# Seven half-size products per pair of token tiles in the second layer's first matmul, and an integer form of the float64 weight decoding

## Chip, cores and metric

One core of a Trainium2 chip runs the whole program. The metric is the time of one execution in device microseconds; the kernel before takes 967.71 us (median of 3 runs, 967.36 to 967.76).

## What is computed

Threshold attention over 4 batches of 8 heads, sequence 576, head size 64, and then two layers on the 2304 x 512 result. The second layer, which the change rewrites, is

```python
h = x @ w_in                                   # 2304x512 @ 512x1024
e = np.exp(h - h_max)
solu = h * (e / (np.sum(e, axis=-1, keepdims=True) + 1e-09))
ln = (solu - mu) / np.sqrt(var + 1e-06) * g_ln  # mu, var: over the 1024 columns of a token
return (ln @ w_out).astype(np.float32)          # 2304x1024 @ 1024x512
```

All four weight matrices arrive as float64 and are turned into float32 on the chip.

## The kernel before, in words

Every matmul operand is kept as a rounded part `hi` and a remainder `lo`, and a product is hi·hi + hi·lo + lo·hi: three matmuls. Their splitting is a copy on ACT and a subtraction on POOL (in a few places on DVE). Each engine works through its own list in the order in which the program text issues it (a hand-written order); between engines only semaphores wait.

**Attention** (until about 360 us) goes through 144 units; weight blocks of 128 x 512 are decoded in between as "jobs", advanced a step at a time by `Jobs.step` (letter J in the table `ORDER`). **Decoding** a block is `words_to_f32` (L506 to L531): the two 32-bit words of a float64 are turned into float32 by one instruction on ACT (L512), five on DVE (L514, L517, L520, L524, L527) and one float addition on POOL (L531). There are 48 blocks; the first 8 go beside attention, 40 beside the first layer.

**First layer** (360 to 757 us): 4 groups of 4 rows of blocks over 5 chunks of tokens (three of 512 columns, two of 384), 80 steps of `moe1_in` (L793) and `moe1_out` (L833), the second 2 steps behind the first. DVE, ACT and POOL clip, square and split each step's result (`moe1_act`), `store_y` adds a finished chunk into `x` (L844), and the jobs load weights of the next group, of which `w_in2` goes partly, `w_out2` wholly, through a float32 copy in DRAM.

**Second layer** (757 us on): 18 token tiles of 128, one after the other. `moe2_in(i)` is 48 matmuls of 512 columns (4 row blocks, 3 matmuls, 2 halves of the 1024 columns; L877) into two PSUM banks. `moe2_ln(i)` reads these banks: DVE takes the row maximum of each half (L893), ACT the two exponentials (L897), DVE multiplies and sums (L905), ACT squares and sums (L910), DVE and POOL (L913) form the inverse deviation, DVE scales (L917). Then the tile is transposed: `moe2_shuffle` does blocks on DVE (L932) and the rest by five DMAs through DRAM, `moe2_land` splits what came back (L951, L952); tiles 0 and 17 go through TensorE instead (`moe2_tr`, L964, `ON_PE`). `moe2_out(i)` is 24 matmuls (L988), one bank, an ACT copy (L992) and a store. In the middle the order is in(i+3), out(i), in(i+4), out(i+1), and so on (the list `seq`):

```python
    seq = [("out", 0)]
    for i in range(1, NTT - 3):
        seq += [("in", i + 3), ("out", i)]
    seq += [("out", NTT - 3), ("tr", NTT - 1), ("out", NTT - 2), ("out", NTT - 1)]
```

Of the kernel before, what the change touches and what calls it, by code (L numbers as in the profile page):

```python
# [21 lines left out]
def kernel(  # L22
# [16 lines left out]
    P = 128  # L39
# [56 lines left out]
    ON_PE = (0, NT // P - 1)  # L96
# [3 lines left out]
    EVERY = (3, 3, 3, 2, 2, 2)  # L100
    X_LEAD = 2
    IN2_AHEAD = (2,)
# [403 lines left out]
    def words_to_f32(raw, n, got):  # L506
# [3 lines left out]
        au, cu = a.bitcast(U32), upper  # L510
        c = cu.bitcast(F32)
# [13 lines left out]
        if fine[0]:  # L525
            yield 1, "b"
# [95 lines left out]
    def block(key, n):  # L622
# [5 lines left out]
        if what == "in2":  # L628
            return (w_in2_f if n in IN2_AHEAD else w_in2)[rows, cols]
# [125 lines left out]
    x_t = {}  # L755

# [101 lines left out]
    def y_split(c, kk):  # L858
        if kk == 0:
            tag = f"x{4 - c % 2 if c else 2}"  # L860
            x_t["y", c] = [xs_p.tile([P, KD, YT * P], F32R, tag=tag + t, name="y") for t in ("h", "l")]
        hi, lo = (t[:, kk, :] for t in x_t["y", c])
        xv = x[:, kk, c * YT * P : (c + 1) * YT * P]
        nc.scalar.copy(hi, xv)
        nc.gpsimd.tensor_tensor(lo, xv, f32(hi), op=ALU.subtract)

    def moe2_in(i):
        r = slice(i % YT * P, i % YT * P + P)
        yh, yl = (t[:, :, r] for t in x_t["y", i // YT])
        ps = [bank("h", (turns[0] + n) % NHB, "h") for n in ((1, 2) if i % 2 else (0,))]  # L870
        if i % 2 == 0:
            ps.append(y_bank(0, "h"))
        n = 0
        for kk in range(KD):
            for a, s in ((yh, 0), (yh, 1), (yl, 0)):
                for g in range(2):
                    nc.tensor.matmul(  # L877
                        ps[g], lhsT=a[:, kk, :], rhs=wg_t["in2", g][s][:, kk, :],
                        start=(n < 2), stop=(n >= 6 * KD - 2),
                    )  # L880
                    n += 1
        h2_ps[i] = ps

    def moe2_ln(i):
        ps = h2_ps.pop(i)
        st = g_p.tile([P, 10], F32, tag="st", name="st", bufs=2)
# [284 lines left out]
```

## Time and profile before

| | |
|---|---|
| median of 3 runs | 967.71 us |
| the profiled execution, its span | 968.04 us, 966.3 us |
| PE busy (5299 matmuls) | 944.8 us, 98% |
| DVE / ACT / POOL busy | 74% / 51% / 62% |
| attention, first layer, second layer | about 360, 397 and 209 us |

Shares of busy time are means over the three stages; the rows below are by stage, and where one number stands for many rows the row is that of a view that groups them.

### The profile page before, as it was taken

How to read it: one execution, taken by the hardware profiler on the slowest of the kernel's cores; microseconds unless marked ns; L12 is line 12 of the kernel's file. 1: busy time of each engine (PE TensorE's matmuls, PEld its weight loads, DVE VectorE, ACT ScalarE, POOL GpSimd, SP SyncE). 2: the span in 40 equal slices, each digit the busy share in tenths (PEclk: the TensorE clock that was granted, in tenths of full speed). 3: DMA queues.
4: the chain of work that ended last, by engine and by line, in shares of the span. 5: the costliest groups of instructions: out<-in, count | busy, mean ns of one | idle time of the engine just before them, and what ended most of it. 6: DMA issues, size and time to landing. Idle time of an engine off the chain costs nothing.

```text
span 966.3 us, 15184 instructions
## 1 busy us (share of the span) xinstructions
PE 944.8 (98%) x5299; PEld 842.3 (87%) x5299; DVE 711.9 (74%) x1132; ACT 493.9 (51%) x924; POOL 603.3 (62%) x575
## 2 busy tenths in 40 slices
PE   7999999999999989999999999999999999999998
PEld 7899899999989978889888988898889988888886
DVE  5788888788788875898678876888675676666562
ACT  3667677777767675354333433333334444344433
POOL 7678788888978898677445544654547614334422
PEclk9999999999999999999999999999999999999999
DMA  6665666657666314211311131112311124444443
GB/s 144 148 147 124 152 159 145 170 126 176 157 142 154 81 44 98 68 66 44 120 44 66 44 119 45 65 45 77 129 34 45 44 66 131 109 120 124 138 119 90
DMA packets 89726, 99.61 MB, mean 103 GB/s; under 512 B 50000, under 2 KB 62608, under 8 KB 89648
## 3 DMA queue, kind: packets, MB, share of 16 engines
q1 hardware_dynamic: 87952, 97.97, 38.5%
q8 instruction: 42, 0.69, 0.3%
q10 hardware_dynamic: 1696, 0.66, 0.3%
q14 instruction: 36, 0.29, 0.1%
HBM read 55.13 MB, written 15.88 MB: 73 GB/s over the span
## 4 chain that ended last, share of the span: by engine, by line
PE 79%; POOL 8%; issue 4%; DVE 4%; ACT 3%; DMA 1%; ACTq 0%; POOLq 0%; DVEq 0%
PE y L833 18%; PE h L793 18%; PE o L988 10%; PE h L877 10%; PE av L453 9%; PE zt L403 6%; PE sc L326 6%; POOL plo L430 3%; PE tr L271 1%; POOL wg L560 1%; DMA nat<-in_q_dram 1%; DVE mcol L339 1%; POOL dec_a L531 1%; POOL xl L769 1%; ACT phi L429 1%
## 5 line engine op out<-in xcount | busy, mean ns | idle before, releaser
L430 POOL TENSOR_TENSOR plo<-e,phi 128x576 fp32r<-128x576 f32 x144 | 207.6, 1451 | 48.9 <-ACT phi L429 48.8
L816 POOL TENSOR_TENSOR gl<-cl,gh 128x512 fp32r<-128x512 f32 (+1 forms) x80 | 100.3, 1254 | 160.0 <-ACT gh L815 85.3
L793 PE MATMUL h<-xh,wg 128*128 128x512 f32 (+1 forms) x640 | 184.1, 369 | 0.7 <-DVE e L421 0.7
L833 PE MATMUL y<-gh,wg 128*128 128x512 f32 (+1 forms) x640 | 184.6, 369 | 0.0
L421 DVE SCALAR_TENSOR_TENSOR e<-zt,ntau,e 128x576 f32<-128x576 f32 x144 | 117.3, 815 | 54.5 <-ACT e L416 34.8
L793 PEld LDWEIGHTS h<-xh,wg 128*128 128x128 f32 x640 | 118.4, 188 | 16.7 <-DVE e L421 1.0
L833 PEld LDWEIGHTS y<-gh,wg 128*128 128x128 f32 x640 | 118.5, 188 | 15.9
L416 ACT ACTIVATE e<-zt 128x576 f32<-128x576 f32 x144 | 93.9, 652 | 70.0 <-PE zt L403 53.2
L339 DVE TENSOR_REDUCE mcol<-sc 128x1 f32<-128x576 f32 x160 | 116.7, 748 | 4.9 <-PE sc L326 4.7
L833 PE MATMUL y<-gl,wg 128*128 128x512 f32 (+1 forms) x320 | 118.8, 371 | 0.9 <-POOL gl L816 0.9
L793 PE MATMUL h<-xl,wg 128*128 128x512 f32 (+1 forms) x320 | 117.8, 368 | 0.0
L815 ACT CAST gh<-cl 128x512 fp32r<-128x512 f32 (+1 forms) x80 | 46.3, 579 | 111.9 <-DVE cl L814 110.7
L812 ACT ACTIVATE cl<-cl,half 128x512 f32<-128x512 f32 (+1 forms) x80 | 54.4, 679 | 95.4 <-DVE cl L811 95.4
L988 PE MATMUL o<-wg,ln 128*128 128x512 f32 x432 | 102.7, 393 | 0.0
L877 PE MATMUL h<-wg,y 128*128 128x512 f32 x432 | 101.1, 390 | 0.0
L988 PEld LDWEIGHTS o<-wg,ln 128*128 128x128 f32 x432 | 80.9, 188 | 18.8 <-ACT ln L951 0.4
L429 ACT CAST phi<-e 128x576 fp32r<-128x576 f32 x144 | 96.2, 668 | 1.5 <-ACT mt L369 0.7
L952 POOL TENSOR_TENSOR ln<-land,ln 128x1024 fp32r<-128x1024 f32 x16 | 38.5, 2404 | 91.7 <-ACT ln L951 85.0
L877 PEld LDWEIGHTS h<-wg,y 128*128 128x128 f32 x432 | 81.0, 188 | 16.8
L811 DVE TENSOR_SCALAR cl<-h 128x512 f32<-128x512 f32 (+1 forms) x80 | 50.6, 632 | 51.1 <-PE h L793 49.0
L326 PE MATMUL sc<-k_both,q_st 128*128 128x288 f32 x320 | 72.2, 307 | 6.5 <-issue 1.8
L403 PE MATMUL zt<-q_st,k_both 128*128 128x288 f32 x320 | 72.4, 308 | 1.6 <-DVE lo L280 1.3
(114 smaller groups left out, 1883.2 us busy)
## 6 DMA issues: line engine op xcount, KB each, us to landing
raw<-in_moe_w_in_dram SPq DMA_DIRECT2D x24, 512.0 KB
raw<-in_moe_w_out_dram SPq DMA_DIRECT2D x24, 512.0 KB
k_both<-q_st SPq DMA_DIRECT2D x30, 288.0 KB
sq<-so SPq DMA_DIRECT2D x64, 128.0 KB
land<-sq SPq DMA_DIRECT2D x16, 512.0 KB
k_both<-lo SPq DMA_DIRECT2D x32, 144.0 KB
q_st<-lo SPq DMA_DIRECT2D x32, 144.0 KB
x<-xs SPq DMA_DIRECT2D x32, 144.0 KB
```

Of the source, the lines that this page charges most:

```text
L326: nc.tensor.matmul(ps[:, c, 0:HS], lhsT=st[j][i][r, n * P : n * P + P], rhs=kk[j][i][r, o + c * HS : o + (c + 1) * HS], start=(st is q_st) ...
L339: nc.vector.tensor_reduce(mc[:, n : n + 1], sc_ps.pop((h, n))[:, :, 0:HS], axis=AXES.XY, op=ALU.max, negate=True)
L403: nc.tensor.matmul(ps[:, c, 0:HS], lhsT=st, rhs=mv[:, c * HS : (c + 1) * HS], start=(m == 0), stop=(m == len(todo) - 1),)
L416: nc.scalar.activation(out=e, in_=st_ps[u][:, :, 0:HS], func=ACTF.Exp)
L421: nc.vector.scalar_tensor_tensor(out=e, in0=st_ps.pop(u)[:, :, 0:HS], scalar=ntau[:, 0:1], in1=e, op0=ALU.is_ge, op1=ALU.mult)
L429: nc.scalar.copy(hi, e)
L430: (nc.vector if u - NU in LO_DVE or u < NU - UNITS and u % UNITS in LO_UNITS else nc.gpsimd).tensor_tensor(lo, e, f32(hi), op=ALU.subtract)
L793: nc.tensor.matmul(ps, lhsT=a[:, kk, f], rhs=m[:, kk, :], start=(n == 0 and kk == 0), stop=(n == 2 and kk == KD - 1),)
L816: nc.gpsimd.tensor_tensor(gl, cl, f32(gh), op=ALU.subtract)
L833: nc.tensor.matmul(y_ps[c][d], lhsT=a[:, jj, ds_], rhs=m, start=(jj == 0 and n == 0), stop=(jj == JG - 1 and n == 2),)
L877: nc.tensor.matmul(ps[g], lhsT=a[:, kk, :], rhs=wg_t["in2", g][s][:, kk, :], start=(n < 2), stop=(n >= 6 * KD - 2),)
L988: nc.tensor.matmul(ps, lhsT=a[:, f, :], rhs=wg_t["out2", f // 4][m][:, f % 4, :], start=(n == 0), stop=(n == len(terms) - 1))
```

## The change

In the second layer two neighbouring token tiles form a 2 x 2 block matrix: rows by tile, columns by halves of the 512 inputs; `w_in2` is cut in the same way into B11, B12, B21, B22. The Winograd form of Strassen's scheme gives the pair's four results from seven products of a 128 x 256 by a 256 x 512 block, 6 matmuls each, with sums of blocks as operands.

- `op_rows` reads `w_in2` (all of it now decoded ahead into DRAM) and forms three of its blocks and four sums of them, each split into hi and lo: 8 subtractions on DVE, 14 copies on ACT, 14 subtractions on POOL, in the first layer's last group. `out2` is split later than before.
- `y_adds` forms four sums of blocks of `x` per pair (DVE); `y_split` splits four pieces per pair, 1792 columns in place of 1024.
- `product(k, n)` is one of the seven. They add up in three banks; the partial results 1, 5 and 6 are copied out by ACT, after 2, 3 and 7 DVE adds the bank to such a copy and takes the row maximum in the same instruction, and after 4 it takes the maximum from the bank. So a later product on a bank waits for ACT or DVE to have read it.
- `moe2_ln` finds three of a pair's four halves in SBUF instead of PSUM. Tiles 1 and 16 go through TensorE too. All operands lie in one large tile `xs` cut by offsets; the order is written out by hand for pairs 0 to 2 and the tail, with a loop for pairs 3 to 8.
- Decoding is now two instructions on ACT, three on DVE and one addition of 32-bit integers on POOL.

```diff
-    ON_PE = (0, NT // P - 1)
+    ON_PE = (0, 1, NT // P - 2, NT // P - 1)
...
-        nc.vector.tensor_scalar(au, au, 3, 0x3FFFFFF8, op0=ALU.logical_shift_left, op1=ALU.bitwise_and)
+        nc.vector.tensor_scalar(au, au, 3, None, op0=ALU.logical_shift_left)
+        nc.scalar.activation(out=lower.bitcast(F32), in_=lower, func=ACTF.Copy, bias=2.0, scale=2.0 ** -51)
...
         nc.vector.scalar_tensor_tensor(
-            out=au, in0=upper, scalar=0xC0000000, in1=au, op0=ALU.bitwise_and, op1=ALU.bitwise_or
-        )
-        yield 1, "s"
-        nc.vector.tensor_scalar(cu, au, 0xFF800000, None, op0=ALU.bitwise_and)
...
-        nc.vector.scalar_tensor_tensor(
-            out=c, in0=lower, scalar=2.0 ** -52, in1=c, op0=ALU.mult, op1=ALU.mult
+            out=au, in0=upper, scalar=0x80000000, in1=au, op0=ALU.bitwise_and, op1=ALU.bitwise_xor
         )
...
-        nc.gpsimd.tensor_tensor(a, a, c, op=ALU.add)
+        nc.gpsimd.tensor_tensor(au, au, lower, op=ALU.add)
...
+    def y_adds(k):
+        r0, r1, pairs = y_views(k)
+        a11, a12, a21, a22 = (x[:, h : h + KH, r] for r in (r0, r1) for h in (0, KH))
+        s1, s2, s3, s4 = (t[:, h : h + KH, :] for t in pairs for h in (0, KH))
+        nc.vector.tensor_tensor(s1, a21, a22, op=ALU.add)
+        nc.vector.tensor_tensor(s3, a11, a21, op=ALU.subtract)
+        nc.vector.tensor_tensor(s2, s1, a11, op=ALU.subtract)
+        nc.vector.tensor_tensor(s4, a12, s2, op=ALU.subtract)
...
+    PRODUCTS = {
+        1: (0, 0, B11), 2: (1, 1, B21), 3: (2, 5, B22), 4: (0, 6, T4), 5: (2, 2, T1), 6: (0, 3, T2), 7: (0, 4, T3),
+    }
...
+    def add_max(i, g, ps):
+        h = so_half(i, g)
+        nc.vector.tensor_tensor_reduce(
+            out=h, in0=ps, in1=h, scale=1.0, scalar=-3.0e38, op0=ALU.add, op1=ALU.max, accum_out=maximum(i, g)
+        )
+
+    def product(k, n):
+        b, a, o = PRODUCTS[n]
+        hi, lo = y_t[k, a]
+        w = op_tile(o)
+        ps = acc(k, b)
+        first = n in (1, 2, 5)
+        for kk in range(KH):
+            for m, (st, at_) in enumerate(((hi, kk), (hi, KH + kk), (lo, kk))):
+                nc.tensor.matmul(
+                    ps, lhsT=st[:, kk, :], rhs=w[:, at_, :],
+                    start=first and kk == 0 and m == 0, stop=kk == KH - 1 and m == 2,
+                    skip_group_check=not first,
+                )
...
+    for k in range(3, NPR):
+        o = 2 * k - 4
+        last = k == NPR - 1
+        if k > 3:
+            product(k - 1, 7)
+        ln_step(o + 2)
+        moe2_fetch(o + 2)
+        product(k, 1)
+        moe2_store(o - 1)
+        product(k, 5)
+        product(k, 2)
+        product(k - 1, 4)
+        moe2_land(o + 1)
+        ln_step(o + 3)
...
+        ln_step(o + 3)
+        if not last:
+            y_adds(k + 1)
+        ln_step(o + 3)
+        moe2_fetch(o + 3)
+        if not last:
+            for m in range(4):
+                y_split(k + 1, m)
+        if k > 3:
+            moe2_out(o)
+            product(k, 6)
+        product(k, 3)
+        moe2_store(o)
+        moe2_land(o + 2)
+        ln_step(2 * k)
...
+        ln_step(2 * k)
+        moe2_out(o + 1, slice(12 * last, None))
```

DVE's list before, one tile of the second layer (`h` a PSUM half, `st` columns of statistics, `so` the tile's result):

```order
L893 TENSOR_REDUCE st<-h 128x1 x2
L894 TENSOR_TENSOR st<-st 128x1
L901 TENSOR_SCALAR st<-st 128x1
L902 RECIPROCAL st<-st 128x1
L905 SCALAR_TENSOR_TENSOR so,st<-h,st,so 128x512 x2
L909 TENSOR_SCALAR st<-st 128x1
L912 TENSOR_SCALAR st<-st 128x1
L914 TENSOR_SCALAR st<-st 128x1
L915 TENSOR_SCALAR st<-st 128x1
L916 TENSOR_TENSOR st<-st 128x1
L917 TENSOR_SCALAR so<-so,st 128x1024
L932 STREAM_TRANSPOSE so<-so 128x8x4x32
```

DVE's list after, in the loop, from `add_max` behind product 2 into the odd tile's `moe2_ln` (`ISA` is the adding and maximum instruction and the read of its result, `mx` the maxima, `x` the sums of `y_adds`):

```order
L975 ISA so,mx<-h,so 128x512
L975 ISA mx 128x1
L1006 TENSOR_REDUCE mx<-h 128x1
L1015 TENSOR_SCALAR st<-mx 128x1
L1022 TENSOR_SCALAR st<-st 128x1
L1023 RECIPROCAL st<-st 128x1
L1026 SCALAR_TENSOR_TENSOR so,st<-h,st,e 128x512
L1026 SCALAR_TENSOR_TENSOR so,st<-so,st,e 128x512
L1030 TENSOR_SCALAR st<-st 128x1
L938 TENSOR_TENSOR x<-x 128x2x128
L939 TENSOR_TENSOR x<-x 128x2x128
L940 TENSOR_TENSOR x<-x 128x2x128
```

Of a pair's four maxima three have moved into adding instructions, and the four sums stand between the odd tile's L1030 and its next step (L1033); the even tile's remaining steps go on as before.

PE's list after, one turn of the loop from product 1 of pair 6 to its product 7 (`h_9486` is the bank of pair 5's product 4, `o` an output bank):

```order
L987 MATMUL h_9664<-op_8137,xs_5363 128x512 x6
L987 MATMUL h_9676<-op_8162,xs_5363 128x512 x6
L987 MATMUL h_9684<-op_8182,xs_5363 128x512 x6
L987 MATMUL h_9486<-xs_5363 128x512 x6
L1132 MATMUL o_9739<-xs_5363,ln_8707 128x512 x24
L987 MATMUL h_9664<-op_8202,xs_5363 128x512 x6
L987 MATMUL h_9676<-op_8222,xs_5363 128x512 x6
L1132 MATMUL o_9795<-xs_5363,ln_8995 128x512 x16
L1132 MATMUL o_9795<-xs_5363,ln_8996 128x512 x4
L1132 MATMUL o_9795<-xs_5363,ln_8997 128x512 x4
L987 MATMUL h_9664<-op_8247,xs_5363 128x512 x6
```

Where 24 matmuls of one tile alternated with 24 of an output, products 1, 5, 2, the pair before's 4, an output, 6, 3, an output and 7 follow each other; product 4 shares its bank with product 7, 24 matmuls earlier.

POOL's list at the end of attention, before and then after (`plo` the attention's remainders, `gl` and `xl` or `xs` those of the first layer, `dec_a` and `wg` a decoded block and its remainder):

```order
L430 TENSOR_TENSOR plo<-e,phi 128x576 x6
L500 TENSOR_TENSOR x<-x,rb 128x576
L430 TENSOR_TENSOR plo<-e,phi 128x576 x2
L531 TENSOR_TENSOR dec_a<-dec_a,raw 128x512
L560 TENSOR_TENSOR wg<-dec_a,wg 128x512
L816 TENSOR_TENSOR gl<-cl,gh 128x512
L769 TENSOR_TENSOR xl<-x,xh 128x512 x2
```

```order
L429 TENSOR_TENSOR plo<-e,phi 128x576 x6
L499 TENSOR_TENSOR x<-x,rb 128x576
L429 TENSOR_TENSOR plo<-e,phi 128x576 x2
L873 TENSOR_TENSOR gl<-cl,gh 128x512
L826 TENSOR_TENSOR xs<-x,xs 128x512 x2
```

The last decoded block's two instructions no longer stand here; with fewer steps in a job all eight blocks are through earlier in attention.

## Rows read from the trace of the kernel before

**Rows 1.** Busy time by stretch: span and busy us (instructions) per engine, TensorE clock, DMA.

```profile
360.00:757.70 397.70, 396.12 (x1909) 347.60 (x1910) 302.85 (x441) 158.65 (x273) 236.94 (x183) 1.00 0.22 69
800.00:940.00 140.00, 140.00 (x614) 114.89 (x613) 88.19 (x211) 59.10 (x118) 52.46 (x40) 1.00 0.46 123
```

**Rows 2.** Chain of waits, second layer: start us, us, what, number of matmuls.

```profile
763.21 2.10 PE y L833 x12
...
784.71 5.54 PE o L988 x24
790.25 5.44 PE h L877 x24
```

**Rows 3.** Timeline, second layer, PE: start us, us, engine, what.

```profile
823.03 5.61 PE L877 MATMUL h<-wg,y 128*128 128x512 f32 x24
```

**Rows 4.** Timeline, DVE, one tile from maximum to the next maximum.

```profile
834.30 1.25 DVE L893 TENSOR_REDUCE st<-h 128x1 f32<-128x512 f32 x2
835.58 0.16 DVE L894 TENSOR_TENSOR st<-st 128x1 f32<-128x1 f32 x1
837.32 0.21 DVE L901 TENSOR_SCALAR st<-st 128x1 f32<-128x1 f32 x1 [1.58 <-ACT so L897]
...
839.24 0.21 DVE L909 TENSOR_SCALAR st<-st 128x1 f32<-128x1 f32 x1
840.82 0.15 DVE L912 TENSOR_SCALAR st<-st 128x1 f32<-128x1 f32 x1 [1.37 <-ACT so L910]
...
842.20 0.58 DVE L916 TENSOR_TENSOR st<-st 128x1 f32<-128x1 f32 x1
...
843.66 1.25 DVE L932 STREAM_TRANSPOSE so<-so 128x1024 f32<-128x1024 f32 x1
844.83 1.25 DVE L893 TENSOR_REDUCE st<-h 128x1 f32<-128x512 f32 x2
```

**Rows 5.** A POOL instruction beside it, and durations (min/median/max ns) of two DVE lines.

```profile
841.75 1.02 POOL L865 TENSOR_TENSOR y<-x,y 128x384 fp32r<-128x384 f32 x1
...
L916 DVE TENSOR_TENSOR st<-st x18: 159/568/580, 773.3 to 947.9; 128x1 f32<-128x1 f32 x18
L917 DVE TENSOR_SCALAR so<-so,st x18: 811/814/1476, 773.5 to 948.1; 128x1024 f32<-128x1024 f32 x18
```

**Rows 6.** Durations by line, min/median/max ns.

```profile
L905 DVE SCALAR_TENSOR_TENSOR so<-h,st,so x36: 745/750/753, 767.5 to 944.1; 128x512 f32<-128x512 f32 x36
L844 DVE TENSOR_TENSOR x<-x,y x60: 544/686/690, 489.3 to 775.6; 128x512 f32<-128x512 f32 x36, 128x384 f32<-128x384 f32 x24
L769 DVE TENSOR_TENSOR xl<-x,xh x4: 1165/1186/1929, 354.3 to 360.6; 128x512 fp32r<-128x512 f32 x4
L556 DVE TENSOR_SCALAR wf<-wf,g_sb x8: 582/830/1242, 736.3 to 762.2; 128x512 f32<-128x512 f32 x8
L531 POOL TENSOR_TENSOR dec_a<-dec_a,raw x48: 1296/1330/1830, 77.3 to 738.4; 128x512 f32<-128x512 f32 x48
```

**Rows 7.** Timeline, a tile's last way through DRAM.

```profile
938.83 1.25 DVE L932 STREAM_TRANSPOSE so<-so 128x1024 f32<-128x1024 f32 x1
...
948.00 1.06 ACT L951 CAST ln<-land 128x1024 fp32r<-128x1024 f32 x1 [1.03 <-DMA land<-sq]
```

**Rows 8.** Timeline, tail: a wait for a landed tile, a transpose on TensorE, its copies.

```profile
943.98 5.39 PEld L988 LDWEIGHTS o<-wg,ln 128*128 128x128 f32 x24 [0.44 <-ACT ln L951]
949.65 1.04 PE L964 MATMUL lt<-ident,so 128*128 128x128 f32 x8
...
950.34 1.08 ACT L965 CAST ln<-lt 128x512 fp32r<-128x512 f32 x2
```

**Rows 9.** Busy time by stretch at the end of attention, and a decoding instruction there.

```profile
340.00:350.00 10.00, 8.50 (x61) 7.66 (x60) 4.02 (x6) 7.22 (x15) 9.86 (x11) 1.00 0.21 56
350.00:365.00 15.00, 13.64 (x84) 11.30 (x82) 12.95 (x13) 9.37 (x16) 14.77 (x10) 1.00 0.13 34
...
341.99 1.29 POOL L560 TENSOR_TENSOR wg<-dec_a,wg 128x512 fp32r<-128x512 f32 x1
```

More of the change, by code (lines that the diff above doesn't have):

```diff
@@ L856 @@
     nc.vector.memset(mhalf, -0.5)
[L858 to L882, printed above, removed]
@@ new lines, with y_home, y_views @@
+    y_t = {}
+    keep = {"y": []}
+    def y_home(k, m):
+        if k % 2 and m < 3:
+            if m == len(keep["y"]):
+                home = g_ps[(turns[2] + m) % len(g_ps)]
+                keep["y"].append([home.tile([P, T], F32R, tag=t, name="y", bufs=1) for t in ("gh", "gl")])
+            return keep["y"][m]
+        o, w = (Y_ODD, PIECE // 4) if k % 2 else (Y_EVEN[m], PIECE // 2 if m < 3 else PIECE // 4)
+        return [xs_part(o + n * w, w) for n in range(2)]
+    def y_views(k):
+        r0, r1 = (slice((2 * k + n) * P, (2 * k + n + 1) * P) for n in range(2))
+        if k:
+            return r0, r1, [x[:, :, (2 * k - 2 + n) * P : (2 * k - 1 + n) * P] for n in range(2)]
+        return r0, r1, [t.rearrange("p (k t) -> p k t", k=KD) for t in keep["s"]]
@@ new lines, with acc, so_half, maximum @@
+    acc_t = {}
+    max_t = {}
+    def acc(k, n):
+        if (k, n) not in acc_t:
+            acc_t[k, n] = y_bank(n, "h") if k % 2 else bank("h", (turns[0] + n) % NHB, "h")
+        return acc_t[k, n]
+    PRODUCTS = {
+        1: (0, 0, B11), 2: (1, 1, B21), 3: (2, 5, B22), 4: (0, 6, T4), 5: (2, 2, T1), 6: (0, 3, T2), 7: (0, 4, T3),
+    }
+    def so_half(i, g):
+        return keep["so"][i // 2 % 2][:, i % 2, g * HF : g * HF + HF]
+    def maximum(i, g):
+        if i not in max_t:
+            max_t[i] = g_p.tile([P, 2], F32, tag="mx", name="mx", bufs=4)
+        return max_t[i][:, g : g + 1]
@@ L895, in moe2_ln @@
+    def moe2_ln(i):
+        st = g_p.tile([P, 10], F32, tag="st", name="st", bufs=3)
+        e = keep["e"][:, i % 2, :]
+        so = keep["so"][i // 2 % 2][:, i % 2, :]
+        half = [slice(HF * g, HF * g + HF) for g in range(2)]
+        h = [so[:, half[0]] if i % 2 == 0 else acc_t[i // 2, 0], so[:, half[1]]]
+        nmax, sm, mu, va, rs, t1 = (st[:, n : n + 1] for n in range(6))
+        nc.vector.tensor_scalar(nmax, maximum(i, 0), maximum(i, 1), -1.0, op0=ALU.max, op1=ALU.mult)
         two = [st[:, n : n + 1] for n in range(8, 10)]
@@ L897, in moe2_ln @@
             nc.scalar.activation(
[L898 removed]
+                out=e[:, half[g]], in_=h[g], func=ACTF.Exp, bias=nmax, scale=1.0, accum_out=two[g]
             )
@@ new lines @@
+    ln_step(0)
+    product(0, 4)
+    product(1, 1)
+    product(1, 5)
+    ln_step(1)
+    y_adds(2)
+    product(1, 2)
+    ln_step(0)
+    product(1, 6)
+    for m in range(2):
+        y_split(2, m)
+    ln_step(1)
+    product(1, 3)
+    product(1, 7)
+    moe2_tr(0)
+    ln_step(1)
+    for m in range(2, 4):
+        y_split(2, m)
+    jobs.finish()
+    ln_step(2)
+    product(2, 1)
+    ln_step(2)
+    ln_step(2)
+    moe2_fetch(2)
+    product(2, 2)
+    product(1, 4)
+    moe2_out(0)
```

327 lines of the change are left out of this document (227 added, 100 removed).

## Prediction

> **What bounds the kernel now.** I read the busy time by stretch first, then the chain of waits, then one tile of the second layer on the timeline. By stretch the reader sees that PE is the bound from the first layer on: 396.12 of 397.70 us busy between 360 and 757.7, all of 140 between 800 and 940, the granted clock at 1.00, its upper level [rows 1]. In the second layer the chain of waits is PE alone: 24 matmuls of `in` take 5.44 us, 226.7 ns each, 24 of `out` 5.54 us (230.8 ns), 12 of the first layer's end 2.10 us [rows 2]. So a tile costs 10.98 us, a pair 21.96, and a matmul less is time gained, as long as the other engines keep up.
>
> They barely do. The product that PE begins at 823.03 ends at 828.64 [rows 3], but DVE takes its maximum only at 834.30, as soon as the tile before is through; from that maximum to the next are 10.53 us [rows 4]. DVE is "63% busy" there (88.19 of 140 [rows 1]), yet a tile occupies its list for 10.53 of PE's 10.98 us, since it waits in line for ACT's exponentials (1.58 us), ACT's squares (1.37) and POOL. **The chip has 0.45 us per tile to spare on DVE, and the change asks PE to be 0.68 us per tile faster.** That decides this case.
>
> **Removed from PE.** Six matmuls fewer per pair (42 for 48), 9 pairs: 54 x 226.7 ns = **-12.24 us**. Whether six in a row on one bank go at 226.7 ns or at the 230.8 of `out`, 24 in a row on one bank, changes this by 378 x 4.1 ns = 1.6 us at most; I take 226.7 and keep 1.6 for the range.
>
> **Added on PE.** Tiles 1 and 16 are now transposed there, 1.04 us for 8 [rows 8]: **+2.1 us**. In exchange 10 DMAs on the sync queue and two DVE transposes go, off the path except for DVE's share below. At the end, out(17) now follows its transposes directly: from their start 0.69 us to the copy, 1.08 us for two copies [rows 8], so some 0.69 + 0.55 + 0.2 - 1.04 = 0.4 us of wait; the wait of 0.44 for a landed tile [rows 8] goes. Zero together. Transfers keep their cover otherwise: transpose to landed copy is 948.00 - 940.08 = 7.9 us [rows 7], and in the new order DVE has about 10 us of work between a tile's transpose and the exponentials queued on ACT behind that tile's copy.
>
> **DVE's list in the loop.** Its pieces come from the tile [rows 4]: maximum known to exponentials done 1.74; from there to the squares' start 1.92; squares 1.58; last small steps, scaling and block transpose 843.66 + 1.17 - 840.82 = 4.01, of which 0.42 is L916 standing at 0.58 instead of its fastest 0.16 because POOL is inside L865 [rows 5]; 3.59 without. New are three add-and-maximum instructions. Nothing like them is in the trace; the nearest row is L905, also one bank, one SBUF operand and an accumulator, 0.75 us [rows 6]. Bounds: a plain addition from a bank, 0.69 (L844), and one with two SBUF operands, 1.19 (L769). One maximum of 0.65 stays. The four sums of 256 columns: L844 takes 0.544 for 384 and 0.686 for 512 columns, 1.1 ns a column, so 0.40 each, 1.6 in all (upper bound half of L769: 2.4). They fill the wait for the odd tile's squares, and one add-and-maximum that for the even tile's. A pair: odd tile 0.75 + 0.65 + 1.74 + 1.92 + (0.21 + 1.6) + 3.59, even tile 0.75 + 1.74 + 1.92 + 1.58 + 3.59, together 20.0 us; with one POOL wait of 0.42 per pair (POOL's splits of the next pair now follow its power directly, on odd tiles) **20.4 us against PE's 42 x 0.2267 + 48 x 0.2308 = 20.6**. So in the loop DVE just keeps up: **0**.
>
> **DVE's list before the loop.** Here it does not. Put 0 at product 1 of pair 0. PE would finish the first layer's last matmuls at 12.3, and DVE their addition and a weight scaling (0.58, L556 [rows 6]) at 13.65. From there it never waits for PE again: tile 0 to 21.4 (just ahead of PE's transposes at 21.8), tile 1 with two add-and-maximum and the two remainders of tile 0 to 29.3, tile 2 in 8.83 to 38.1, an add-and-maximum, a maximum, tile 1's remainders (2 x 0.69) and tile 3 to 50.6, tile 4 to 59.4, tile 5 with the sums to 69.9, tile 6 up to its squares to 74.3, and the add-and-maximum behind product 7 of pair 3 to 75.2. Three POOL waits of 0.42 (tiles 1, 3 and 5, where splits follow) make it 76.5. Product 4 of pair 3 uses that bank; PE, unhindered, starts the loop at 44.6 (20 products of 1.36, two steps of 2.1 of the first layer, two outputs of 5.54, two transposes of 1.04) and is at the gate at 44.6 + 4 x 1.36 + 5.54 + 2 x 1.36 + 5.54 + 4 x 1.36 = 69.3. **PE waits 7.2 us in sum, +7.2**, partly at that gate, partly already at product 1 of pair 4 (its operand is split after DVE's sums) and at out(3). This is the lag that DVE already has today, which a slower PE hid.
>
> **ACT and POOL in the loop.** Per pair ACT gains three bank copies and longer splits, POOL 768 columns of splitting; ACT was busy 59.10 and POOL 52.46 of 140 us [rows 1]. Both are covered by more than half of the time; what counts is where they stand in DVE's way, which is above.
>
> **Decoding and loading.** Two DVE instructions per block go and one on ACT comes. For the 40 blocks of the first layer and for `op_rows` this is free: PE is at 396.12 of 397.70 with DVE at 302.85 and POOL at 236.94 [rows 1]; a step of 12 + 12 matmuls lasts 5.4 us, in which POOL's one remainder and two operand splits take three times about 1.3. The price of an integer addition on POOL is not in the trace; from L531's fastest 1.30 us to twice its 1.33 [rows 6] it stays hidden there; a quicker one would gain nothing. Beside attention it matters: from 340 to 365 us POOL is busy 24.63 of 25 us and PE only 22.14, so 2.86 us are missing [rows 9]. Decoding's POOL instructions of 1.3 us, one at 341.99 and a last pair behind the attention's end, leave this stretch. I take half of the missing time, **-1.4 us** (bounds -2.9, and +2 if the integer addition takes twice as long).
>
> **Sum.** -12.24 + 2.1 + 0 + 7.2 + 0 - 1.4 = -4.3 us. The profiled execution took 968.04 us, 0.33 more than the median of 967.71; so 963.7 profiled, **963.4 us as a median**. A difference below 0.2%, 1.9 us, counts as none: it is about what can be told from no change.
>
> **The rule against it.** In rows 5 L916, with two SBUF operands, takes 580 instead of 159 ns while POOL runs, and L917 1476 instead of 811. The Trainium skill (GPSIMD Engine Reference, Key points) says that GpSimd shares its SBUF interfaces with VectorE and contends with instructions in a 2-port mode or with two SBUF inputs. The trace agrees by these two lines. By that rule the change makes DVE more exposed, and the first rival below follows.
>
> **Rivals.** *DVE becomes the bound of the whole layer (slower).* Three of a pair's four multiplications (L1026) and the four sums now read two SBUF operands, where before one was a bank. If each multiplication and the first sum met a POOL instruction as L916 does (0.42), a pair would take 20.4 + 4 x 0.42 = 22.1 us. Three pairs' worth before the gate add 5.0, and four turns at 1.5 over PE add 6.0: 963.4 + 11.0 = 974; met half the time, 21.25 us: 2.5 + 4 x 0.65 = 5.1, **968.5**. It passes from gain to loss near 21.1 us a pair. For it: POOL goes from 37% to about half busy and works in bursts of 5 us. Against: the multiplications stand mostly where POOL waits for ACT.
>
> *DVE is quicker than I add up (more gain).* Steps that wait for each other here may overlap when a second pair's work stands between. If the gate costs 2 instead of 7.2, **958.2**; with no wait at all 956.2. Against: the order leaves DVE little to put into its waits for exponentials.
>
> *Nothing comes of it.* The matmuls go, and the waits of PE grow by as much: gate 10 to 11 us, so **967**. The same if products on one bank go at 230.8 ns and attention gains nothing (963.4 + 1.6 + 1.4 = 966.4).
>
> **Chances.** The forecast, gate of 5 to 9 us and the loop covered, 961.5 to 965.8: 0.35, faster. Nothing comes of it: 0.22, same. More gain: 0.23, faster. DVE the bound: 0.20, slower. So faster 0.58, same 0.22, slower 0.20. The range takes in most of both sides: from a gate of about 1.5 us, 957.5, to DVE halfway met and a slow add-and-maximum on top (0.2 us x 7 pairs), 970.
>
> **What would show it.** Right: 378 matmuls at `product`'s line near 226.7 ns a step; PE's first long wait just before product 4 of pair 3, released by DVE's add-and-maximum, and together about 7 us of waits up to there; from then on hardly any; turns of 20.6 us; DVE's turn a little below that. Wrong: waits in every turn with DVE never idle (the slower rival), or no wait at that gate (more gain); add-and-maximum far from 0.75 us; the 340 to 365 stretch unchanged.

## The result, and the profile after

The changed kernel takes **972.99 us** (median of 6 runs, 971.94 to 977.17), the kernel before 967.57 in the same session: ratio **1.0062** (95% interval 1.0045 to 1.008), slower by 5.4 us. The forecast was 963.4 with a range up to 970.0, so it was wrong in size and in sign. The profiled execution took 973.01 us, its span 971.2 us, 4.9 more than before; the forecast had asked for 4.3 less.

First the busy time by stretch (span, then busy us and instructions of PE, its weight loads, DVE, ACT, POOL; TensorE's clock, DMA), against [rows 1] and [rows 9]:

```profile
340.00:350.00 10.00, 9.59 (x72) 9.31 (x71) 6.08 (x8) 7.07 (x15) 9.08 (x13) 1.00 0.16 47
350.00:365.00 15.00, 12.94 (x92) 11.88 (x91) 10.54 (x12) 12.88 (x24) 14.49 (x10) 1.00 0.15 42
360.00:757.70 397.70, 396.44 (x1921) 348.64 (x1920) 252.81 (x375) 184.06 (x320) 236.68 (x184) 1.00 0.23 77
...
800.00:850.00 50.00, 43.48 (x179) 33.90 (x178) 35.88 (x96) 26.64 (x53) 21.90 (x21) 0.97 0.45 125
850.00:900.00 50.00, 50.00 (x218) 40.68 (x217) 36.54 (x90) 27.50 (x55) 29.10 (x26) 1.00 0.42 117
```

PE is still the busy engine nearly everywhere, but for one hole: 6.5 us are missing between 800 and 850, and of these stretches only that one has a granted clock below 1.00. PE's timeline of the second layer shows the hole (start us, us, instruction, in brackets the idle time before it and what ended it):

```profile
759.71 5.68 PE L987 MATMUL h<-op,xs 128*128 128x512 f32 x24
...
778.28 4.44 PE L987 MATMUL h<-op,y 128*128 128x512 f32 x18 [0.38 <-ACT so L994]
...
817.82 3.05 PE L987 MATMUL h<-op,y 128*128 128x512 f32 x12 [1.18 <-ACT so L994]
...
828.07 0.73 PE L987 MATMUL h<-op,xs 128*128 128x512 f32 x2 [0.15 <-ACT xs L948]
829.68 3.94 PE L987 MATMUL h<-op,xs 128*128 128x512 f32 x16 [0.88 <-POOL xs L949]
837.92 2.38 PE L987 MATMUL h<-xs 128*128 128x512 f32 x6 [4.30 <-DVE mx L975]
840.11 6.53 PE L1132 MATMUL o<-xs,ln 128*128 128x512 f32 x24
...
861.81 5.61 PE L1132 MATMUL o<-xs,ln 128*128 128x512 f32 x24
...
882.51 5.60 PE L1132 MATMUL o<-xs,ln 128*128 128x512 f32 x24
...
903.30 5.61 PE L1132 MATMUL o<-xs,ln 128*128 128x512 f32 x24
...
948.41 11.33 PE L1132 MATMUL o<-xs,ln 128*128 128x512 f32 x48 [1.25 <-ACT o L1142]
...
960.85 5.76 PE L1132 MATMUL o<-xs,ln 128*128 128x512 f32 x24 [0.24 <-ACT ln L1108]
```

The wait of 4.30 us is the gate that was forecast: product 4 of pair 3, released by the add-and-maximum (L975). With 0.38 at 778.28 the waits up to there add to 6.9 us; 7.2 had been forecast. Behind it something came that had not: product 4 takes 2.19 us to the next start where it takes 1.40 later, the output 6.36 instead of 5.45, together 1.70 us. The granted clock is 0.93 from 830 to 840 and 0.90 from 840 to 850, so part of this stretch ran at 1.2 instead of 2.4 GHz, right after PE had stood still. The two rows account for the loss: 10 x (0.07 + 0.10) = 1.7 us. From then on PE goes without a wait of DVE, output to output in 20.70 to 20.79 us, as forecast (20.6).

That looks as if DVE kept up in the loop. Its own timeline says otherwise; one turn of it:

```profile
866.40 0.21 DVE L1022 TENSOR_SCALAR st<-st 128x1 f32<-128x1 f32 x1 [1.55 <-ACT e L1018]
...
870.72 0.27 DVE L1035 TENSOR_SCALAR st<-st 128x1 f32<-128x1 f32 x1 [0.67 <-POOL st L1034]
...
871.22 0.75 DVE L1037 TENSOR_TENSOR st<-st 128x1 f32<-128x1 f32 x1
872.01 1.75 DVE L1038 TENSOR_SCALAR so<-so,st 128x1024 f32<-128x1024 f32 x1
...
882.28 0.16 DVE L1037 TENSOR_TENSOR st<-st 128x1 f32<-128x1 f32 x1
882.48 0.81 DVE L1038 TENSOR_SCALAR so<-so,st 128x1024 f32<-128x1024 f32 x1
...
887.56 0.21 DVE L1022 TENSOR_SCALAR st<-st 128x1 f32<-128x1 f32 x1 [1.55 <-ACT e L1018]
```

POOL's timeline beside it:

```profile
870.14 0.55 POOL L1034 TENSOR_TENSOR st<-st,mhalf 128x1 f32<-128x1 f32 x1 [4.79 <-DVE st L1033]
870.65 4.96 POOL L949 TENSOR_TENSOR xs<-x,xs 128x512 fp32r<-128x512 f32 x4
```

From 866.40 to 887.56 DVE's turn is **21.16 us**, longer than PE's 20.75, and it never waits for PE. Its last two steps of the odd tile, L1037 and L1038, take 0.75 and 1.75 us while POOL makes the remainders of the next pair's operands, 0.16 and 0.81 for the even tile, where POOL is idle: 1.53 us per pair. The forecast had 0.42.

The prices of the new instructions came out near their estimates (min/median/max ns):

```profile
L975 DVE CUSTOM_DVE_ANT_0 so<-h,so x27: 650/679/694, 764.2 to 937.8; 128x512 f32<-128x512 f32 x27
L938 DVE TENSOR_TENSOR x<-x x8: 414/416/423, 764.8 to 910.8; 128x256 f32<-128x256 f32 x8
L523 POOL TENSOR_TENSOR dec_a<-dec_a,raw x48: 1295/1316/1894, 58.3 to 679.3; 128x512 uint32<-128x512 uint32 x48
```

Finally, the second layer starts at 759.71 us, before it was 757.56: the first two stages became 2.15 us longer, where 1.4 less was forecast. To place this I follow one landmark, attention's 31 matmuls of the identity with the tile `mr`, the last of them near its end (the range is that of their starts, first to last). In the kernel before:

```profile
L363 PE MATMUL zt<-ident,mr x31: 273/273/275, 27.2 to 345.6; 128*10 128x128 f32 x31
```

In the changed one:

```profile
L362 PE MATMUL zt<-ident,mr x31: 273/273/275, 28.6 to 350.7; 128*10 128x128 f32 x31
```

The landmark's last start is 5.1 us later; of that some 1.4 are there already at its first start, from a transfer that landed later before any decoding. From the landmark to the second layer it is 409.0 us instead of 411.95.

### The profile page after: what moved, and what is told of

It reads as the page before. It is cut to its first block, busy times and chain, and to the rows that moved or that the text cites. A ratio compares the mean times of both kernels' runs of the same rounds, so it can differ in the third digit from the quotient of the medians.

```text
span 971.2 us, 15226 instructions
## 1 busy us (share of the span) xinstructions
PE 939.4 (97%) x5261; PEld 836.4 (86%) x5261; DVE 661.8 (68%) x1109; ACT 543.7 (56%) x1019; POOL 623.8 (64%) x605
## 5 line engine op out<-in xcount | busy, mean ns | idle before, releaser
L873 POOL TENSOR_TENSOR gl<-cl,gh 128x512 fp32r<-128x512 f32 (+1 forms) x80 | 97.2, 1216 | 152.1 <-ACT gh L872 92.6
L850 PE MATMUL h<-xs,wg 128*128 128x512 f32 (+1 forms) x768 | 164.4, 362 | 0.0
L850 PEld LDWEIGHTS h<-xs,wg 128*128 128x128 f32 x768 | 139.6, 188 | 16.3
L1132 PE MATMUL o<-xs,ln 128*128 128x512 f32 x432 | 103.7, 395 | 1.6 <-ACT o L1142 1.2
L1132 PEld LDWEIGHTS o<-xs,ln 128*128 128x128 f32 x432 | 81.6, 190 | 21.1 <-ACT o L1142 1.5
L452 PE MATMUL av<-phi,v_hi 128*128 128x288 f32 x320 | 71.3, 304 | 1.8 <-ACT xs L464 1.8
L523 POOL TENSOR_TENSOR dec_a<-dec_a,raw 128x512 uint32<-128x512 uint32 x48 | 65.8, 1371 | 8.3 <-DVE dec_a L519 5.5
L452 PE MATMUL av<-plo,v_hi 128*128 128x288 f32 x320 | 69.4, 298 | 1.3 <-POOL plo L429 1.3
L452 PE MATMUL av<-phi,v_lo 128*64 128x288 f32 x320 | 69.4, 298 | 0.0
```

The costliest lines, as they stand in the source:

```text
L452: nc.tensor.matmul(ps[0:o, c, 0:HS], lhsT=vv, rhs=pp[:, c, :], start=first and pp is hi and o == P, stop=last and pp is lo,)
L850: nc.tensor.matmul(ps, lhsT=a[:, kk, f], rhs=m[:, kk, :], start=(n == 0 and kk == 0), stop=(n == 2 and kk == KD - 1),)
L873: nc.gpsimd.tensor_tensor(gl, cl, f32(gh), op=ALU.subtract)
L1132: nc.tensor.matmul(o_ps[i], lhsT=a[f], rhs=wg_t["out2", f // 4][m][:, f % 4, :], start=(n == 0), stop=(n == len(terms) - 1))
```

## The experiments

Two questions: which of the losses in the second layer is the cause (the gate and the clock behind it, or DVE's rate), and what the decoding does to attention. **My theory:** DVE, collided with by POOL, bounds the second layer. **Rival:** the loop has slack, and the gate with its slower clock is the loss. The session of each run has its own runs of the kernel before (medians 967.5, 967.9, 968.6 and 968.5), so ratios are given. Ratios of different sessions are not comparable to better than 0.003, some 3 us: e4, e7, e8 and e14 leave the second layer as long as the changed kernel does (211.5 to 211.9 us from its start to the end of the span, 211.5 there), and yet their ratios are 1.0053, 1.0032, 1.0034 and 1.0038 for its 1.0062. Where it matters, neighbours of one session or the second layer's length in the profiles are compared.

**The decoding, alone and taken out.** e1 is the kernel before with the new `words_to_f32`, e2 the changed kernel with the old one.

> The kernel before with the new decoding alone. In the profile of the changed kernel the second layer begins 1.9 us later than before, though 1.4 us earlier was forecast. If the decoding does that (fewer steps, so its work falls at other places beside attention): 967.6 + 1.9 = 969.5 us. If it is the chance of one execution (a transfer that landed 1.5 us later at 13.8 us, before any decoding): 967.6, within 0.7. If the prediction's term holds: 967.6 - 1.4 = 966.2.

> The changed kernel with the decoding of before. If the new decoding costs 1.9 us: 973.0 - 1.9 = 971.1. If the late start was chance: 973.0. If the prediction's term holds: 974.4. In the second layer all say: waits and turns as in the changed kernel.

e1: 970.9 us, ratio 1.0032 (1.0021 to 1.0044): the decoding alone makes the kernel before slower by 3.1 us. Its landmark in that view:

```profile
L363 PE MATMUL zt<-ident,mr x31: 272/273/275, 27.2 to 351.8; 128*10 128x128 f32 x31
```

e2: 974.62 us, 1.0078 (1.0066 to 1.009). By the time that is the third expectation (974.4), but its interval overlaps with the changed kernel's, so it isn't told from 973.0 either, and the way there was none of the three. Its landmark:

```profile
L362 PE MATMUL zt<-ident,mr x31: 273/273/276, 27.0 to 344.6; 128*10 128x128 f32 x31
```

The landmark is back at 344.6 us, but from there to the second layer it now takes 415.0 us, and that layer starts at 759.60, where the changed kernel's does. In these single profiles, then, the new decoding costs some 6 us up to the landmark (351.8 for 345.6, 350.7 for 344.6) and behind it saves 3.0 (e1: 409.0 for 411.95) to 6.0 us (changed kernel: 409.0 for 415.0). With the old decoding the operands of the seven products, called free in the prediction, cost 3.0 us behind the landmark (415.0 for 411.95). The term has two halves of opposite sign; the forecast saw a part of the second one only. That it is a loss in sum is shown in the kernel before, not in the changed one.

**POOL's part in DVE's turn.** In e3 POOL doesn't work beside those two steps from the fifth pair on:

```diff
-        nc.gpsimd.tensor_tensor(lo, v, f32(hi), op=ALU.subtract)
+        if k < 4:
+            nc.gpsimd.tensor_tensor(lo, v, f32(hi), op=ALU.subtract)
```

> The changed kernel; from the fifth pair on POOL's remainder of the operands is left out (stale values stand in its place), so POOL doesn't work just when DVE does the last steps of the odd tile. Collision theory: these two DVE steps go back from 0.75 and 1.75 to 0.16 and 0.81 us, DVE's turn from 21.17 to 19.6 us; before the gate one such tile lies, so the wait of 4.3 us falls to 2.8 and the time to 971.5, and with a shorter wait the clock may stay up (up to 1.9 more, 969.6). Rival, the steps are long for another reason (two operands on a moving scalar, DVE's own state): durations, gate and time unchanged, 973.0.

969.87 us, 1.0026 (1.0011 to 1.0042), 3.1 us under the changed kernel and 2.5 under e4 of the same session. The profiled execution is one of its longer ones (972.33 us); its second layer takes 209.6 us, 1.9 less than the changed kernel's. DVE's timeline (its lines are one number higher here):

```profile
870.12 0.16 DVE L1038 TENSOR_TENSOR st<-st 128x1 f32<-128x1 f32 x1
870.31 0.81 DVE L1039 TENSOR_SCALAR so<-so,st 128x1024 f32<-128x1024 f32 x1
```

and what DVE waited for from 850 to 935 us (us in total, times, longest):

```profile
DVE so L976 <- PE h L988: 3.9, 4, 1.1
DVE mx L1007 <- PE h L988: 2.3, 4, 0.6
```

Both steps are short again, and DVE waits 6.2 us for PE in four turns, where in the changed kernel it waited for PE not once. That POOL's remainders make these steps long is shown; the other reason is refuted. The gate opened 1.5 us sooner, 76.7 instead of 78.2 us after the second layer's start (837.58 - 760.89, and 837.92 - 759.71); the wait fell only to 4.0 us, since PE arrived sooner too, no longer held up by POOL.

**PE kept busy at the gate.** e4 lets PE do 20 matmuls twice:

```diff
         product(k, 2)
+        if k == 4:
+            moe2_out(o, slice(0, 20), True)
         product(k - 1, 4)
```

> The changed kernel; just before product 4 of pair 3 PE does 20 matmuls of the next output once more (their result is thrown away), 4.6 us, so that it is busy where it waited 4.3 us. If the slower matmuls after the gate (0.97 granted in that stretch) are lost time, and the loop has slack: clock 1.00 there and 973.0 - 1.9 + 0.3 = 971.4. If DVE bounds the loop (its turn 21.17 us against PE's 20.75): the clock is 1.00, but PE then waits some 0.4 us in each of the next four turns, released by DVE, and the time stays at 973.0 within 0.4.

972.35 us, 1.0053 (1.0041 to 1.0065). The clock is 1.00 throughout the second layer, and nothing is gained: from the start of the second layer to the end of the span it is 211.5 us as in the changed kernel. PE's timeline, outputs behind the gate:

```profile
839.13 5.61 PE L1132 MATMUL o<-xs,ln 128*128 128x512 f32 x24
...
860.29 5.60 PE L1132 MATMUL o<-xs,ln 128*128 128x512 f32 x24
...
881.45 5.60 PE L1132 MATMUL o<-xs,ln 128*128 128x512 f32 x24
...
902.62 5.60 PE L1132 MATMUL o<-xs,ln 128*128 128x512 f32 x24
...
923.78 5.62 PE L1132 MATMUL o<-xs,ln 128*128 128x512 f32 x24
```

Every turn is now 21.16 or 21.17 us: DVE's turn, to the hundredth. The time, 0.6 us under the changed kernel, lies between the two expectations and does not decide; the turn does. Of the expected waits the profile shows only 0.3 us in all, but the pace is DVE's. So in the changed kernel the slower matmuls behind the gate gave DVE a lead of 1.7 us, which it used up again at 0.4 us a turn; that is why PE showed no wait. The rival falls.

**The output ahead at one gate.** e7 moves `moe2_out(4)` ahead of product 4 of pair 3:

```diff
         product(k, 2)
+        if k == 4:
+            moe2_out(o)
         product(k - 1, 4)
...
-        if k > 3:
+        if k > 4:
             moe2_out(o)
+        if k > 3:
             product(k, 6)
```

> The changed kernel; at the gate the output of tile 4 goes ahead of product 4 of pair 3, so PE has 5.5 us of work where it waited 4.3 us. If the gate and the clock after it were the loss: 973.0 - 4.3 - 1.9 = 966.8. If DVE bounds the layer (turn 21.17 us): the wait of 4.3 us goes, PE then waits as much again at the next gates, each released by DVE, and the time is 972 to 973.

972.39 us, 1.0032 (1.0019 to 1.0044) in a session in which e8 below, which changes nothing that matters, gave 971.67: no gain. The wait at the gate is gone; on PE's timeline the next one stands at 850.65 us:

```profile
838.46 1.52 PE L987 MATMUL h<-xs 128*128 128x512 f32 x6
...
850.65 2.29 PE L987 MATMUL h<-op,xs 128*128 128x512 f32 x6 [2.28 <-ACT so L1000]
852.73 5.31 PE L987 MATMUL h<-op,y 128*128 128x512 f32 x18
```

The copy that releases it stands in ACT's list behind the exponentials and the square of tile 7, which wait for DVE, and behind the copies of the next pair's splits; the clock drops again (0.83 from 850 to 860).

**A product's 232 ns.** In e8 two products at a time alternate, matmul by matmul, between two banks (`two`):

```diff
-        product(k, 1)
+        two(k, 1, k, 5)
         moe2_store(o - 1)
-        product(k, 5)
-        product(k, 2)
-        product(k - 1, 4)
+        two(k, 2, k - 1, 4)
```

> The changed kernel; in the loop products 1 and 5, and 2 and the last pair's 4, go alternately, matmul by matmul, on two banks. If one bank in a row is what makes a product's matmul 232 ns: 24 such matmuls take 5.44 instead of 5.57 us. If a new weight for each matmul does it: 5.57 as before. In both cases DVE bounds the loop and the time stays at 973.0 within 0.5.

971.67 us, 1.0034 (1.0022 to 1.0045). The 24 alternating matmuls ahead of an output take 861.38 - 855.82 = 5.56 us; in the changed kernel the same 24 take 861.81 - 856.23 = 5.58. One bank in a row is not the reason. Nor does it matter whether two matmuls in a row use the same stationary operand: in `product` the first two of every three do (`hi`), in e8 none do. In the next turn, where the products read `xs` and not `y`, the 24 take 5.49 us in both kernels (882.51 - 877.02 in the changed one), and product 4 there takes 1.36 us, 226.7 ns a matmul. What slows the others stays open.

**Splits spread.** In e6 two of the four splits stand ahead of the odd tile's exponentials, one behind the even tile's landed copy:

```diff
         moe2_land(o + 1)
+        if not last:
+            y_split(k + 1, 0)
+            y_split(k + 1, 3)
         ln_step(o + 3)
...
-            for m in range(4):
-                y_split(k + 1, m)
+            y_split(k + 1, 1)
...
         moe2_land(o + 2)
+        if not last:
+            y_split(k + 1, 2)
```

> The changed kernel; in the loop two of a pair's four operand splits are put ahead of the odd tile's exponentials (DVE is waiting for ACT then) and one behind the even tile's landed copy, so that only one follows POOL's power directly. Collision theory with DVE as the bound: the odd tile's last two steps, 0.75 and 1.75 us, come down to about 0.6 and 1.2, DVE's turn from 21.17 to about 20.3; from pair 4 on that is what leaving the remainders out did (3.1 us less time, 969.9), so part of that: 970.5 to 972. Rival (the collision only moves to the multiplications): turn about 21, time 973.

970.51 us, 1.0027 (1.0014 to 1.004), at the edge of the expected range. It is only 1.2 us under e8 of the same session, with overlapping intervals; what shows the gain is the second layer, 210.0 us for 211.5, in a profiled execution that is the longest of the twelve (974.69 us, with attention longer than in any other profile). DVE's two steps on its timeline, with the even tiles' L1038 for the turn:

```profile
842.39 0.81 DVE L1038 TENSOR_SCALAR so<-so,st 128x1024 f32<-128x1024 f32 x1
...
862.61 0.81 DVE L1038 TENSOR_SCALAR so<-so,st 128x1024 f32<-128x1024 f32 x1
...
872.50 0.74 DVE L1037 TENSOR_TENSOR st<-st 128x1 f32<-128x1 f32 x1
873.28 0.81 DVE L1038 TENSOR_SCALAR so<-so,st 128x1024 f32<-128x1024 f32 x1
```

and on POOL's timeline the split that is left there:

```profile
871.94 1.29 POOL L949 TENSOR_TENSOR xs<-x,xs 128x512 fp32r<-128x512 f32 x1
```

These rows show what sets the length of L1037: it ends when the POOL instruction that it met ends, 872.50 + 0.74 = 873.24 beside 871.94 + 1.29 = 873.23. In the kernel before it was the same, 842.78 for L916 and 842.77 for L865 ([rows 4], [rows 5]). So what L1037 and L916 pay for meeting POOL is what is left of POOL's instruction, however small they are themselves.

PE's timeline at the gate:

```profile
840.18 2.93 PE L987 MATMUL h<-xs 128*128 128x512 f32 x6 [4.74 <-DVE mx L975]
842.90 6.88 PE L1132 MATMUL o<-xs,ln 128*128 128x512 f32 x24
```

DVE's turn (842.39 to 862.61) is 20.2 us, where 20.3 had been expected, and now the gate and the clock behind it are a loss: DVE waits for PE again, 2.7 us in four turns.

**Old pace.** A job is moved on a step at a time; the new decoding has two steps fewer, so blocks follow each other sooner. e5 puts two empty steps back, e9 does the same in the kernel before:

```diff
             out=au, in0=upper, scalar=0x80000000, in1=au, op0=ALU.bitwise_and, op1=ALU.bitwise_xor
         )
+        yield 1, "s"
+        if fine[0]:
+            yield 1, "b"
         yield 1, ""
```

> The changed kernel with the new decoding's instructions, but two empty steps per block, so that a block takes as many steps beside attention as before. The last matmul of attention's masks stands at 345.6 us in the kernel before and at 350.4 to 351.9 in every profile with the new decoding (344.6 with the old one in the changed kernel), though it has fewer instructions. Pace theory (blocks follow each other sooner, so more of DVE's, ACT's and POOL's work falls into the middle of attention, where it makes PE wait): the mark returns to 345 or a little below, the time falls by 3 to 5 us, to 968 to 970. Rival (the integer addition on POOL or the activation on ACT is what makes attention wait): mark stays near 350, time 973.

> The kernel before with the new decoding's instructions at the old number of steps per block, nothing else. With the same decoding in the changed kernel the second layer began at 754.95 us, 2.6 earlier than in the kernel before. Pace theory: so it does here, and nothing takes the gain back in the second layer: 967.6 - 2.6 = 965.0. Rival (in the changed kernel the first layer was shortened by its operand loading, not by the decoding): the gain is near 0, 967.5.

e5: 970.09 us, 1.002 (1.0004 to 1.0036). Its landmark:

```profile
L362 PE MATMUL zt<-ident,mr x31: 272/273/275, 27.1 to 344.9; 128*10 128x128 f32 x31
```

and the second layer starts at 754.95 us. That speaks for the pace of the new instructions, and not their price, as what made attention longer. Over all profiles: with the new decoding at its own pace the landmark lies at 348.8 to 353.9 us (8 profiles, middle 350.5), at the old pace at 343.8 to 349.4 (7 profiles, middle 347.5). Part of the overlap goes with TensorE's granted clock. Summed over rows of 10 us up to 350 us, 10 x (1 - clock) is 0 in e5, e9 and e10, 1.7 or 3.4 us in most others, 5.1 in e12 and 6.8 in e6. With that taken off, an estimate, the landmark lies at 347.1 to 350.1 us at the new pace and at 343.8 to 345.9 at the old one, and the two no longer overlap. e9: 967.77, ratio 0.9992 (0.9975 to 1.0009), below e1's 1.0032 (another session), so at the old pace the new instructions cost nothing. But the expected gain of 2.6 us is not there by the interval, though the profiled execution had it (second layer at 753.90 us, 965.04 us): attention's length scatters between executions by several microseconds, and why the clock drops in some of them stays open.

**Together.** e10 is old pace, spread splits, and output 13's copy ahead of the last tile's exponentials on ACT; e11 adds the order of e7 with product 6 right behind; e12 adds the splits of pairs 2 and 3 at other places. The two new edits (e10's, then e12's):

```diff
     ln_step(i)
+    moe2_store(i - 3)
     ln_step(i + 1)
     moe2_land(i - 1)
-    moe2_store(i - 3)
     moe2_out(i - 2)
```
```diff
     product(1, 6)
-    for m in range(2):
+    for m in range(4):
         y_split(2, m)
...
     ln_step(1)
-    for m in range(2, 4):
-        y_split(2, m)
...
     moe2_fetch(3)
+    moe2_land(2)
     for m in range(2, 4):
         y_split(3, m)
-    moe2_land(2)
```

> The changed kernel with three of the edits together: decoding at the old pace (-2.9 measured alone), operand splits spread (-2.5 measured alone), and at the end the copy of output 13 ahead of the last tile's exponentials on ACT (a wait of 1.2 us of PE stands there). If they add up: 973.0 - 2.9 - 2.5 - 1.2 = 966.4, a little below the kernel before. If DVE still bounds the end, the last takes nothing: 967.6.

> The same, and at the gate the output of tile 4 ahead of product 4 of pair 3, product 6 of pair 4 right behind it. With splits spread DVE's turn is 20.2 us, shorter than PE's 20.75, so DVE theory says that the gain at the gate, 4.7 us of wait and the 2 to 3 us of the slower matmuls after it, is now mostly kept, while alone it gave 0.6: 966.4 - 4 to 6 = 960.5 to 962.5. Rival (DVE is behind by more than this order tolerates, the wait comes back at the next product that needs an operand): 965 to 966.5.

> The same, and the splits of pairs 2 and 3 moved off the last steps of tiles 1 and 3 as well (0.74 + 1.19 and 0.97 + 1.19 us there instead of 0.16 + 0.81 each): DVE arrives up to 2.1 us earlier at the gate. If a wait is left there: up to 2 us less than the kernel above. If none is left: the same time.

968.0 us, 0.9998 (0.9986 to 1.001); 968.5, 0.9998 (0.9983 to 1.0013); 968.61, 0.9994 (0.9983 to 1.0005). The three edits of e10 come to 6.2 us by the ratios (1.0062 to 0.9998; 6.6 expected), but to only some 3.4 if e7 or e8 stands for the changed kernel, so that they add up is not shown. The two edits behind gain nothing in the time; in the profiles the second layer is 210.1, 209.7 and 208.3 us. PE's timeline of e11 shows why: the gate has only moved to the next turn, whole.

```profile
855.79 2.92 PE L990 MATMUL h<-xs 128*128 128x512 f32 x6 [4.81 <-DVE mx L978]
```

**The order in every turn.** So e13 keeps the output ahead of product 4 from the fifth pair to the last; e14 does this alone, without the shorter turn; e15 is e13 with e12's splits.

```diff
         product(k, 2)
+        if k > 3:
+            moe2_out(o)
         product(k - 1, 4)
         moe2_land(o + 1)
+        if k > 3:
+            product(k, 6)
...
-        if k > 3:
-            moe2_out(o)
-            product(k, 6)
         product(k, 3)
```

> The kernel of the tenth experiment (old pace, splits spread, output 13's copy earlier), and in every turn from the fifth pair on the output of the even tile ahead of product 4 of the pair before, product 6 right behind that product. Order theory (the loop lets PE be ahead of DVE by so much, one output more makes up for it as long as DVE's turn, 20.2 us, is not longer than PE's 20.75): no wait of 4.8 us at any product 4, no slower matmuls behind it, the second layer 5 to 7 us shorter (from 210 us to 203 to 205), the time 968.0 - 5 to 7 = 961 to 963. Rate theory (DVE sets the end whatever the order): the wait appears elsewhere, 967 to 968.

> The changed kernel with that order of the loop alone; DVE's turn stays at 21.17 us. Order theory: the wait of 4.3 us goes, then DVE falls 0.42 us behind in each of four turns, so at most 1.7 us come back, and the slower matmuls behind the gate go: 973.0 - 4.3 - 1.9 + 1.7 = 968.5, up to 970.5 if the clock drops at one of the later waits. Rate theory: 972 to 973, as when the output went ahead at one gate only (972.4).

> e13 and the splits of pairs 2 and 3 moved as in the twelfth experiment. Order theory: no gate is left for DVE's earlier arrival to shorten, so the time is that of e13 within 0.5 us. Rate theory: up to 2 us less than e13.

e13: 966.4 us, **0.9969** (0.9956 to 0.9982). e14: 973.01, 1.0038 (1.0025 to 1.0052). e15: 965.49, **0.996** (0.9944 to 0.9976). What is left at the last product 4, on PE's timeline of e13:

```profile
933.91 2.15 PE L990 MATMUL h<-xs 128*128 128x512 f32 x6 [2.60 <-DVE mx L978]
```

And of e14:

```profile
937.54 2.93 PE L987 MATMUL h<-xs 128*128 128x512 f32 x6 [3.66 <-DVE mx L975]
```

The second layer, from its start to the end of the span, takes 206.9 us in e13 and 211.8 in e14 (changed kernel 211.5, kernel before 208.7). It needs both: with the turn at 21.16 us the order alone gains nothing, and PE goes from output to output in 21.1 to 21.2 us; with the turn at 20.2 it goes at its own 20.74, and the order lets it run ahead by one output, so that the gate is not met until the tail. All profiles say the same of DVE's turn: the second layer takes 211.5 to 212.0 us in the seven kernels that leave it at 21.16 (the changed one, e2, e4, e5, e7, e8, e14), whatever they do at the gate, and 206.4 to 210.1 in the seven that shorten it (e3, e6, e10 to e13, e15). e13's second layer stayed 1.9 us and more above its expectation since that last gate remained, with slower matmuls behind it (clock 0.83 from 930 to 940); the rest of its distance lies ahead of the second layer (759.21 us, e10 755.04). e15's gain over e13 lies within the intervals, so the early splits are not shown to matter. e15 and e13 beat both kernels of this case.

## Why the prediction was wrong

- **Removed and added on PE.** The matmuls went as counted. Their size was off: products at 1.36 to 1.40 us for 6, some 232 ns each, instead of 226.7; over 378 that is +2.0 us where 0 was taken and 1.6 kept for the range.
- **The gate before the loop.** Right in releaser and mostly in place: 4.30 us at the gate and 1.03 at product 1 of pair 4, as said; 1.56 came behind ACT's copies of a bank (L994), none at out(3). The size, 6.9 us for 7.2, is in part luck. The gate opens 78.2 us after the second layer's start, where 76.5 had been put, since the two steps of tiles 1, 3 and 5 are 3.7 us over and 1.3 had been put; and PE without its earlier waits of 2.6 us would have been there at 71.3, where 69.3 had been put.
- **DVE's list in the loop: "just keeps up, 0".** This step failed. Its pieces were right (without collisions a turn is 21.16 - 1.53 = 19.6 us, 20.0 forecast), but one POOL wait of 0.42 was put in where the splits of four operands, 5 us of POOL, lengthen two steps by 1.53. PE's and DVE's turns had been put at 20.6 and 20.4; they are 20.75 and 21.16, so the sign of their difference, on which the term stood, was wrong. The hint was in [rows 5]: L917's longest is 1476 instead of 811 ns, and only L916's 0.42 went into the sum.
- **The slower matmuls behind the gate**, 1.7 us, were not in the sum. e4 shows that in the changed kernel they cost nothing beyond DVE's rate; in e6, with DVE quicker, they do.
- **The tail, "zero together".** 1.25 us of wait came: output 15 needs a bank whose copy is queued on ACT behind the last tile's exponentials. In e10, which moves the copy, the wait is gone; it is gone in e6 too, which doesn't, so an ACT that comes sooner is enough.
- **Decoding and loading, -1.4.** This step failed too: the stages ahead of the second layer became 2.15 us longer in the profile. That the end of attention would be relieved was right, 1.2 us from the landmark to the first layer's first matmul (364.65 - 350.7 for 360.71 - 345.6). Two parts of opposite sign were missed. The first layer, put at "free", became 1.8 us shorter. And a job with fewer steps runs sooner, so that more decoding falls into the middle of attention: 5.1 us later at the landmark, 3 of them (by the middles of the profiles) undone by two empty steps. As a loss in sum the decoding is shown in the kernel before only (e1, 3.1 us).

No single term makes the miss. The span's 9.2 us of error are 3.6 from the first two stages, 2.0 from the products' rate, 1.7 from behind the gate and 1.5 from the tail's two waits, less 0.3 at the gate; 0.7 are not placed. Of the cases, the first rival came nearest, DVE as the bound of the layer, at 0.20. That the time lies within its price of 968.5 to 974 is in part luck: at a turn of 21.16 us its own sum gives 963.4 + 3 x 0.76 + 4 x 0.56 = 967.9, near its turning point, and the other 5 us come from the terms above. Its mechanism was named at the wrong instructions: the multiplications were mostly spared, the two steps behind POOL's power were hit.

The rule weighed in the prediction (the Trainium skill, GPSIMD Engine Reference, Key points: shared SBUF interfaces, contention with a 2-port mode or two SBUF inputs) is borne out by e3: L1037, with two SBUF operands, 0.75 and 0.16 us with and without POOL's remainders. The rival that was worked out from it had the right sign. L1038, which has one SBUF operand and two scalars per partition, was lengthened too (1.75 and 0.81 us); whether the rule covers it, no run here shows.

## What to carry to other kernels

When two engines' turns lie within a few per cent of each other, the forecast hangs on the difference, not on either turn: take the longest durations of a contended row into the sum, not the median, and place each engine's new bursts on the other's timeline. A bound engine is not always seen by waits of its follower: compare the turns themselves, since a follower that was just slowed may hide it. Taking steps out of work that is interleaved by steps changes its pace; hold the pace and change the cost in separate edits.

## What the runs showed that was not expected

- A DVE instruction on 128 x 1 elements took 0.75 instead of 0.16 us and one of 128 x 1024 1.75 instead of 0.81 us while POOL subtracted beside it; the first ended when POOL's instruction ended. Add-and-maximum, which reads one operand from a bank, stayed at 0.65 to 0.69.
- After a wait of 4.3 to 4.9 us TensorE's granted clock was 0.66 to 0.93 in the row of 10 us that holds its end, and 6 matmuls took up to 2.93 us instead of 1.55; filled with 20 extra matmuls the same wait left it at 1.00 (e4).
- An addition of 32-bit integers on POOL costs what the float addition did: 1316 ns beside 1330 [rows 6].
